# A transformer mixer on one core: the second MLP's mixed first weights made in the first MLP's last block and kept in DRAM

## Chip, cores and metric

The kernel runs on one core of a Trainium2 chip. The metric is the device time of one execution in microseconds (us); lower is better. TensorE (PE) does the matmuls, VectorE (DVE), ScalarE (ACT) and GpSimd (POOL) the elementwise work, SyncE (SP) issues nearly all DMAs.

## What is computed

Four sequences of 576 tokens, 8 heads of 64, in fp32. Windowed causal attention, then an MLP behind a layer norm, then a token mixer and a second MLP, each added to its input:

```python
attn = softmax(mask(q @ k.T / 8))            # each row sees itself and 63 keys before it
x  = (attn @ v) as [4, 576, 512]
x  = x + relu(layernorm(x) * g @ wa1) @ wa2  # wa1 512 x 2048, wa2 2048 x 512
u  = x + (relu(x.T @ tok1) @ tok2).T         # tok1 576 x 256, tok2 256 x 576, along the tokens
out = u + relu(u @ wb1) @ wb2                # wb1 512 x 1536, wb2 1536 x 512
```

## The kernel before, in words

**Numbers.** Every matmul operand is split into a high part (rounded to fp32r, on ScalarE) and a low part (source minus high, on VectorE or POOL); a product is three passes, `PASSES` (L358): high x high, high x low, low x high. `split` (L101) does both, `relu_split` (L360) does it behind a relu. The weights come as 64-bit values: `b_load` (L613) loads a piece of 512 KB into a raw buffer, `b_shrink` (L624) rescales its exponents on ScalarE, `b_narrow` (L630) makes fp32 of it by two VectorE instructions (L120, L121; the first into PSUM or, with `psum=False`, into SBUF) and loads the next piece into the raw buffer that came free. There are three raw buffers, parts of `qkv`, which held q, k and v of the attention.

**First MLP.** 18 tiles of 128 tokens in 6 blocks of 3. A block has 16 steps, one for each 128 hidden columns. `mm1` (L365) of step f makes the hidden values (12 matmuls of 384 columns into one of two PSUM banks of `ps_h`, then `relu_split`), `mm2` (L382) adds those of step f - 2 (`LAG` = 2) to three accumulators (9 matmuls of 512 columns). The weights of step f lie in SBUF slot f (`wslot`, L96, slots 0 to 15), so in the last block slot f comes free when `mm2` of f has run, in step f + 2. `hooks[f]` are functions called in step f between `mm1` and `mm2`, `hooks[f - 0.5]` ahead of the relu of step f. The order is written by hand: each engine takes its instructions in the order in which the program calls them, and a new tile in a slot waits for the readers of the old one.

**Last block (i = 5, L742 to L755), before.** Three pieces are loaded at step 0. The token rows `ys` (slots 0 to 4) are split at steps 3 to 7 by `ysk`, highs on ScalarE and lows on VectorE. From step 8 pieces are narrowed and split: tok1 in two (`t1_piece`), tok2 in two (`t2_piece`), rests of both (`rest_piece`), then wb1 and wb2 pieces alternating. `t2_piece` takes slot 6 + a, and clears its pads by memsets on POOL (L552) when its load is issued. At step 12 `mix_w1(0)` runs.

**Mixing.** The second MLP's first product is done on blocks of 2 x 2 with seven products in place of eight. For that each wb1 chunk q (of six) is needed in seven forms: a11, a12, a22 (`w1a`) and four sums m1 to m4 (`w1b`). `mix_w1` (L591) makes them of the narrowed chunk `atmp`: highs and lows of the three plain forms, four sums on VectorE (L598), highs and lows of the sums, and stores both tiles to DRAM (`kept`, L606), 768 KB and 1 MB. `load_w1` (L586) loads them back for the later pairs.

**Token mixing (L773 to L848).** `tok_up(b)` makes the hidden values of sequence b in two halves, with functions called in between, `tok_down(t)` gives tile t's result, which VectorE adds to x (L805). Order: up 0, up 1, down 0 to 8 (with the second half's `ys`, highs on ScalarE and lows on POOL), up 2, up 3, down 9 to 17. Meanwhile u of tiles 0 to 5 is transposed by VectorE in 32 x 32 blocks, 16 instructions for three tiles (`block_transpose`, L342), into two tiles `ut` (slots 15 and 11), and `x_steps` (L829) makes seven combinations of it (`xm`, subtractions on VectorE, then a split each); its first two steps run behind the second half of up 3, the others at down 10 to 14.

**Second MLP (L851 to L1006).** Three pairs of two blocks, each pair in six quads (q = 0 to 5), one for a wb1 chunk q and its wb2 chunk. `quad` (L884) runs seven products (six matmuls of 384 columns each, into two PSUM banks in turn, emptied by ScalarE or VectorE) and, from the second quad on, four `down` products (nine matmuls of 512 columns) of the quad before. `jobs[k]` are functions called at eight places in it. In the first pair (p = 0) job 0 of quad q calls `mix_w1(q + 1)`, and jobs 1, 2, 3 and 5 narrow pieces of wb1 and wb2 and split wb2; four places in slots 15 and 11 (`more`) serve as raw buffers. `turn` transposes the next pair's tiles on VectorE.

Of the kernel before, what the change touches and what calls it, by code (L numbers as in the profile page):

```python
# [68 lines left out]
def mixer_kernel(ctx, tc, qT, kT, v, g, wa1, wa2, tok1, tok2, wb1, wb2, out):  # L69
# [334 lines left out]
    with tc.manual_schedule():  # L404
# [104 lines left out]
        HALF = FB // 2  # L509
        W1_SLOT, W2_SLOT = ((8, 9), (5, 6)), (10, 7, 12, 13, 14, 11)  # L510
        w2, ws1, atmp = {}, {}, {}
        kept = dram.tile([HALF, P, 7 * DM], F32, name="kept")

        def new_ys(pr, k):
            ys[pr, k] = wslot(k, [P, 2, 2, DM], f"ys{pr}_{k}")

# [24 lines left out]
        def t1_piece(k):  # L541
            if k == 0:
                tw["t1"] = wslot(5, [P, 2, 4, T1], "t1")
# [18 lines left out]

        def w2_piece(q, k):
            def parts(w):
                if k == 0:
                    w2[q] = wslot(W2_SLOT[q], [P, 2, 2, DM], f"w2_{q}")
                return [(w, w2[q][:, k, 0], w2[q][:, k, 1])]
            f = q + k * HALF
            return [(ALLP, 0, DM, wb2[f * P:(f + 1) * P, :])], parts

        def w1_piece(q, k):
            f = q + k * HALF
            return [(ALLP, 0, DM, wb1[f * P:(f + 1) * P, :])], (q, k)

# [15 lines left out]

        def mix_w1(q):  # L591

            t_ = atmp.pop(q).rearrange("p k (c n) -> p (k c) n", c=2).bitcast(F32)
            a_, b_ = new_w1(q)
# [12 lines left out]
        pb = [(t1_piece, (k,)) for k in range(2)] + [(t2_piece, (a,)) for a in range(2)] + [(rest_piece, ())]  # L609
        pb += [(fn, (q, k)) for q in range(HALF) for fn in (w1_piece, w2_piece) for k in range(2)]  # L610
        todo_b, ready_b = list(enumerate(pb)), []

# [17 lines left out]
        def b_narrow(psum=True):  # L630
            b_shrink()
            _, k, raw, width, parts = ready_b.pop(0)
            if isinstance(parts, tuple):
                if parts[1] == 0:
                    atmp[parts[0]] = ap.tile([P, 2, DM], U32, tag="p", name=f"atmp{parts[0]}")
                tmp = atmp[parts[0]][:, parts[1]]
# [12 lines left out]
        def b_split():  # L649
            b_shrink()  # L650
# [155 lines left out]

        tok_up(0)
        tok_up(1)
        uts_ = [wslot(k, [P, KD, N], f"ut{i}", F32) for i, k in enumerate((15, 11))]
        parts = [lambda k=k, i=i: block_transpose(uts_[i], i, k) for i in range(2) for k in range(16)]  # L810

# [26 lines left out]

        tt = [ap.tile([P, 2, N], F32, tag="p", name=f"t{k}x") for k in range(2)]
        xs0 = x_steps(uts_[0], uts_[1], *tt, [nc.gpsimd, nc.gpsimd, nc.vector, nc.gpsimd, nc.vector, nc.gpsimd, nc.vector])  # L840
        tok_up(2, [lambda: run(3) for _ in range(4)])
        tok_up(3, [lambda: run(3), lambda: run(4), lambda: run(3), *xs0[0], *xs0[1], lambda: None, lambda: None])
        xm += [wslot(k, [P, 2, 2, N], f"xm{k}") for k in range(5)]
        for t in range(9, 18):
            tok_down(t)
            if 10 <= t < 15:
                for fn in xs0[t - 8]:
                    fn()  # L848


# [99 lines left out]
        for p in range(PAIRS):  # L950
            old, acc_of = acc, {}
            for q in range(HALF):
                n = p * HALF + q
                jobs = collections.defaultdict(list)
                if p == 0:
                    if q == 0:
                        more = [wslot(k, [P, 2, 2 * DM], f"more{k}", U32) for k in (15, 11)]
                        places = [more[k][:, h] for k in range(2) for h in range(2)]
                        order = [[places[k % 4]] for k in range(12)] + [places[0:1], places[1:2], [], places[0:1]]
                        rawb_of = lambda raw: order.pop(0) if order else []  # L960
                    if q < HALF - 1:
                        jobs[0].append(lambda q=q: mix_w1(q + 1))
                        for k in (1, 2):
                            jobs[k] += [lambda: b_narrow(False), b_split]
                        if q < HALF - 2:
                            for k in (3, 5):
                                jobs[k].append(lambda: b_narrow(False))
                if n + 1 >= HALF and n + 1 < PAIRS * HALF:
                    jobs[0].append(lambda n=n: load_w1(n + 1))
                if p < PAIRS - 1:  # L970
                    if q == 0:
# [10 lines left out]
                    if q == HALF - 1:  # L982
                        tx = wslot(15, [P, 2, 2, N], f"tx{p}", F32)
                        steps = x_steps(ux[:, 0], ux[:, 1], tx[:, 0], tx[:, 1], [nc.gpsimd, nc.vector] * 4)
                        for k in range(7):
                            jobs[k] += steps[k]
# [60 lines left out]
```

## Time and profile before

| what | us |
|---|---|
| median of 3 runs | 860.7 (858.77 to 862.88) |
| the profiled execution | 859.97 |
| its span, first to last instruction | 858.2 |
| TensorE busy in the span | 817.1 (95%) |
| VectorE, ScalarE, POOL busy | 572.4, 329.7, 165.4 |
| granted TensorE clock, mean | 0.982 |

All rows are of that one execution; times in a row that names a start count from the span's first instruction. A row with "[x <-ENGINE name]" says that the engine stood idle for x before it and what ended that. A merged row counts several instructions ("x9") from the first's start to the last's end. L numbers are lines of the kernel before.

### The profile page before, as it was taken

The numbers are of one execution on the slowest core, as the hardware profiler recorded it, in microseconds if no ns is written. First come the engines' busy times: TensorE is split into PE (matmuls) and PEld (weight loads), VectorE is DVE, ScalarE is ACT, GpSimd is POOL, SyncE is SP. The second block draws the span as 40 slices with busy tenths as digits, with TensorE's granted clock in tenths as the row PEclk, the third lists the DMA queues.
The fourth block names the chain that finished last, engine by engine and source line by source line (L and its number), as shares of the span: only waits on it lengthen the run. The fifth ranks groups of instructions, "written<-read, shape, count | busy, mean of one in ns | idle before, by whom it ended". The sixth has DMA issues, their size and how long they took to land.

```text
span 858.2 us, 13091 instructions
## 1 busy us (share of the span) xinstructions
PE 817.1 (95%) x4902; PEld 717.9 (84%) x4902; DVE 572.4 (67%) x1352; ACT 329.7 (38%) x844; POOL 165.4 (19%) x171
## 2 busy tenths in 40 slices
PE   8999999999999999999999987778889999999998
PEld 6888898898899898899998865666778889889896
DVE  6888768787786877776374597777787644742213
ACT  6887433334423334422353312533344222422221
POOL 3655300000000000000033403433333000310000
PEclk9999999999999999999999999799989999999999
DMA  9887111102201111200055000555432442244312
GB/s 344 259 293 242 56 62 50 57 2 77 82 1 56 57 56 38 97 27 0 1 167 184 1 0 12 209 184 179 146 153 87 160 172 86 93 151 173 106 67 74
DMA packets 28543, 91.41 MB, mean 107 GB/s; under 512 B 3392, under 2 KB 4416, under 8 KB 26176
## 3 DMA queue, kind: packets, MB, share of 16 engines
q1 hardware_dynamic: 28336, 90.32, 30.4%
q8 instruction: 38, 0.62, 0.3%
q10 hardware_dynamic: 144, 0.26, 0.1%
q14 instruction: 25, 0.20, 0.1%
HBM read 74.84 MB, written 15.73 MB: 106 GB/s over the span
## 4 chain that ended last, share of the span: by engine, by line
PE 81%; DVE 10%; ACT 3%; issue 2%; POOL 2%; DMA 1%; SPq 0%; DVEq 0%; POOLq 0%; ACTq 0%
PE acca L385 23%; PE ha L374 22%; PE accb L867 15%; PE prod L858 13%; PE o L281 2%; DVE ut L347 2%; PE s L188 2%; DVE atmp L598 1%; DVE tmpb L121 1%; PE td L802 1%; PE accb L1003 1%; DVE xs L805 1%; PE th L786 1%; DMA more<-in_wb 1%; POOL w L104 1%
## 5 line engine op out<-in xcount | busy, mean ns | idle before, releaser
L374 PE MATMUL ha<-xnt,wa 128*128 128x384 f32 x1152 | 216.8, 337 | 0.8 <-POOL wa L104 0.5
L385 PE MATMUL acca<-wa,hTa 128*128 128x512 f32 x864 | 215.5, 395 | 0.0
L374 PEld LDWEIGHTS ha<-xnt,wa 128*128 128x128 f32 x1152 | 203.9, 188 | 9.5 <-DVE xnt L339 1.2
L385 PEld LDWEIGHTS acca<-wa,hTa 128*128 128x128 f32 x864 | 159.3, 188 | 32.6 <-issue 2.4
L867 PE MATMUL accb<-w,hx 128*128 128x512 f32 x612 | 158.2, 404 | 0.2 <-DVE xs L941 0.2
L867 PEld LDWEIGHTS accb<-w,hx 128*128 128x128 f32 x612 | 118.3, 195 | 22.4 <-issue 0.5
L361 ACT ACTIVATE hTa<-ha 128x384 fp32r<-128x384 f32 x96 | 46.8, 488 | 217.9 <-PE ha L374 217.8
L362 DVE SCALAR_TENSOR_TENSOR hTa<-ha,hTa 128x384 fp32r<-128x384 f32 x96 | 53.3, 555 | 85.7 <-ACT hTa L361 84.8
L256 DVE STREAM_TRANSPOSE pts<-f 32x256 f32<-32x256 f32 x192 | 83.7, 436 | 3.1
L858 PE MATMUL prod<-xm,w1b 128*128 128x384 f32 x324 | 66.3, 348 | 11.6 <-ACT s L872 11.6
L858 PEld LDWEIGHTS prod<-xm,w1b 128*128 128x128 f32 x324 | 59.1, 193 | 17.5 <-ACT s L872 14.8
L881 DVE SCALAR_TENSOR_TENSOR hx<-s,hx 128x384 fp32r<-128x384 f32 x54 | 35.9, 665 | 45.8 <-ACT hx L878 45.4
L878 ACT ACTIVATE hx<-s 128x384 fp32r<-128x384 f32 x54 | 28.3, 524 | 90.9 <-PE accb L867 87.9
L872 ACT ACTIVATE s<-prod 128x384 f32<-128x384 f32 x72 | 34.7, 488 | 69.2 <-PE prod L858 58.7
L355 DVE STREAM_TRANSPOSE xhT<-xh 32x128 f32<-32x128 f32 x192 | 57.9, 301 | 2.8
L875 DVE TENSOR_TENSOR s<-prod,s 128x384 f32<-128x384 f32 x36 | 20.0, 556 | 58.2 <-PE prod L858 58.0
L858 PE MATMUL prod<-xm,w1a 128*128 128x384 f32 x216 | 47.1, 357 | 8.1 <-DVE s L875 8.1
L305 POOL TENSOR_SCALAR mv<-mv 128x1 f32<-128x1 f32 x13 | 2.6, 196 | 269.4 <-ACT xhT L304 269.3
L858 PEld LDWEIGHTS prod<-xm,w1a 128*128 128x128 f32 x216 | 41.2, 201 | 11.0 <-DVE s L875 9.4
L875 POOL TENSOR_TENSOR s<-s,s 128x384 f32<-128x384 f32 x18 | 19.3, 1073 | 153.8 <-ACT s L872 153.8
L104 POOL TENSOR_TENSOR wa<-tmp,wa 128x512 fp32r<-128x512 f32 x32 | 41.5, 1312 | 34.0 <-ACT wa L103 32.2
L209 ACT ACTIVATE f<-f,mx 128x128 f32<-128x128 f32 x120 | 46.3, 388 | 1.2 <-DVE mx L201 1.2
(165 smaller groups left out, 975.1 us busy)
## 6 DMA issues: line engine op xcount, KB each, us to landing
xs<-in_wa SPq DMA_DIRECT2D x32, 512.0 KB, 4.7
w1b<-kept SPq DMA_DIRECT2D x12, 1024.0 KB, 6.6
w1a<-kept SPq DMA_DIRECT2D x12, 768.0 KB, 4.5
more<-in_wb SPq DMA_DIRECT2D x15, 512.0 KB, 5.7
qkv<-in_v SPq DMA_DIRECT2D x28, 256.0 KB, 3.3
kept<-w1b SPq DMA_DIRECT2D x6, 1024.0 KB, 4.9
qkv<-in_wb SPq DMA_DIRECT2D x9, 512.0 KB, 4.6
kept<-w1a SPq DMA_DIRECT2D x6, 768.0 KB, 3.2
```

The lines of the kernel that those rows point to most:

```text
L104: lo_engine.tensor_tensor(out=dst_lo, in0=src, in1=dst_hi.bitcast(F32), op=ALU.subtract)
L209: nc.scalar.activation(out=f_[:, h], in_=f_[:, h], func=AF.Exp, scale=-1.0, bias=mx[:, h], accum_out=sm[:, h])
L256: nc.vector.transpose(out=s_[32 * b:32 * b + 32, :, 32 * a:32 * a + 32], in_=f_[32 * a:32 * a + 32, :, 32 * b:32 * b + 32])
L355: nc.vector.transpose(out=uts[t][32 * b:32 * b + 32, :, 32 * a:32 * a + 32], in_=s_)
L361: nc.scalar.activation(out=dst_hi, in_=src, func=AF.Relu)
L362: nc.vector.scalar_tensor_tensor(out=dst_lo, in0=src, scalar=0.0, in1=dst_hi.bitcast(F32), op0=ALU.max, op1=ALU.subtract)
L374: nc.tensor.matmul(h_, lhsT=w[:, a, c * P:(c + 1) * P], rhs=src[c][:, b], start=n == 0, stop=n == 3 * KD - 1)
L385: nc.tensor.matmul(acc[j], lhsT=t_[:, a, j * P:(j + 1) * P], rhs=ws[f][:, 2 + b], start=f == first and n == 0, stop=f == last and n == 2)
L858: nc.tensor.matmul(dst, lhsT=w_[:, a, c * P:(c + 1) * P], rhs=xm[m][:, c, b], start=first and n == 0, stop=n == 5, skip_group_check=True)
L867: nc.tensor.matmul(acc[j], lhsT=hx[role][:, a, (j % TPB) * P:(j % TPB + 1) * P], rhs=w2[q][:, k, b], start=q == 0 and role in ("21", "12") ...
L875: eng.tensor_tensor(out=dst, in0=x, in1=y, op=ALU.add)
L881: nc.vector.scalar_tensor_tensor(out=hx[role][:, 1], in0=src, scalar=0.0, in1=hx[role][:, 0].bitcast(F32), op0=ALU.max, op1=ALU.subtract)
```

## The change

The wb1 pieces come first: those of q = 2, 3, 4, 5, 0 (`ORDER`) before the token weights, that of q = 1 behind them, then all wb2 pieces. Three are loaded already in the block before the last (step 13). In the last block every step from 1 to 15 narrows one piece; `mix_w1` is now three functions at three successive steps: `w1_plain` (splits of a11, a12, a22 and the four sums, which go from VectorE to POOL), `w1_mixed` (split of the sums) and `w1_keep` (the store). They use slots 0 to 3. `ys` moves to slots 4 to 8 and to steps 7 to 11, tok1 to slot 9, tok2 to slots 10 and 11. q = 1 is mixed during up 1, and the first wb2 chunk is narrowed and split during up 3 and down 9 to 17. In the first pair W1 of q = 2 to 5 is loaded from DRAM; two narrows and one wb2 split are left in a quad, with two raw places. Of the six tiles' transposes for the first pair, three tiles stay with VectorE and three go to TensorE (`turn1`: 12 transposes of 128 x 128 and four copies on ScalarE). The turns for the next pair are spread as 10, 11, 11 over quads 2 to 4. Cut to its core:

```diff
-        W1_SLOT, W2_SLOT = ((8, 9), (5, 6)), (10, 7, 12, 13, 14, 11)
+        W1_SLOT, W2_SLOT = ((0, 1), (2, 3)), (9, 10, 11, 12, 13, 14)
...
-            t2[a] = wslot(6 + a, [P, 2, 960], f"t2_{a}")
+            t2[a] = wslot(10 + a, [P, 2, 960], f"t2_{a}")
...
-        def mix_w1(q):
+        def w1_plain(q):
+            t_ = wtmp["1", q].rearrange("p k (c n) -> p (k c) n", c=2).bitcast(F32)
+            a_, _ = new_w1(q)
             a11, a12, a21, a22 = (t_[:, k] for k in range(4))
-            sub = lambda out, x, y, op=ALU.subtract: nc.vector.tensor_tensor(out=out, in0=x, in1=y, op=op)
             split(a_[:, 2, 0], a_[:, 2, 1], a22, nc.gpsimd)
             split(a_[:, 0:2, 0], a_[:, 0:2, 1], t_[:, 0:2], nc.gpsimd)
-            sub(a22, a21, a22, ALU.add)
-            sub(a21, a11, a21)
-            sub(a11, a22, a11)
-            sub(a12, a12, a11)
+            for out_, x, y, op in ((a22, a21, a22, ALU.add), (a21, a11, a21, ALU.subtract),
+                                   (a11, a22, a11, ALU.subtract), (a12, a12, a11, ALU.subtract)):
+                nc.gpsimd.tensor_tensor(out=out_, in0=x, in1=y, op=op)
+        def w1_mixed(q):
+            t_ = wtmp.pop(("1", q)).rearrange("p k (c n) -> p (k c) n", c=2).bitcast(F32)
+            b_ = ws1[q][1]
             split(b_[:, :, 0], b_[:, :, 1], t_, nc.gpsimd)
+        def w1_keep(q):
             for x_, k_ in w1_rows(q):
                 nc.sync.dma_start(out=k_, in_=x_)
+        ORDER = (2, 3, 4, 5, 0)
+        pb = [(w_piece, (wb1, "1", q, k)) for q in ORDER for k in range(2)]
+        pb += [(t1_piece, (k,)) for k in range(2)] + [(t2_piece, (a,)) for a in range(2)] + [(rest_piece, ())]
+        pb += [(w_piece, (wb1, "1", 1, k)) for k in range(2)]
+        pb += [(w_piece, (wb2, "2", q, k)) for q in range(HALF) for k in range(2)]
...
+                if i == NBLOCKS - 2:
+                    hooks[FA - 3].append(lambda: b_load(3))
...
-                hooks[0].append(lambda: b_load(3))
                 for k in range(5):
-                    hooks[k + LAG + 1].append(lambda k=k: ysk(k))
-                for f in range(6 + LAG, 12 + LAG):
+                    hooks[k + LAG + 5].append(lambda k=k: ysk(k))
+                for f in range(1, FA):
                     hooks[f - 0.5] = [b_narrow]
-                    hooks[f].append(b_split)
-                    if f != 7 + LAG:
-                        hooks[f] += [b_narrow, b_shrink]
-                hooks[10 + LAG].append(lambda: mix_w1(0))
+                for k, q in enumerate(ORDER):
+                    for x, fn in enumerate((w1_plain, w1_mixed, w1_keep)):
+                        hooks[2 * k + 3 + x].append(lambda q=q, fn=fn: fn(q))
+                for f in range(FA):
+                    hooks[f] += [b_split, b_shrink] if f > 10 else [b_shrink]
...
-        tok_up(0)
-        tok_up(1)
+        tok_up(0, [b_split, lambda: b_narrow(), b_shrink, lambda: b_narrow()])
+        tok_up(1, [lambda: w1_plain(1), lambda: w1_mixed(1)])
...
+        turn1((0, 1))
+        tok_up(2, [lambda: turn1((2, 3)), lambda: run(3), lambda: run(3), b_shrink])
+        tok_up(3, [*xs0[0], *xs0[1], b_narrow, lambda: None, lambda: None, lambda: None])
...
+            if t == 12:
+                b_narrow()
+            if t == 15:
+                w2_split(0)
...
-                        jobs[0].append(lambda q=q: mix_w1(q + 1))
-                        for k in (1, 2):
-                            jobs[k] += [lambda: b_narrow(False), b_split]
-                        if q < HALF - 2:
-                            for k in (3, 5):
-                                jobs[k].append(lambda: b_narrow(False))
-                if n + 1 >= HALF and n + 1 < PAIRS * HALF:
+                        for k in (0, 2):
+                            jobs[k].append(b_shrink)
+                            jobs[k + 1].append(lambda: b_narrow(False))
+                        jobs[5].append(lambda q=q: w2_split(q + 1))
+                if 2 <= n + 1 < PAIRS * HALF:
                     jobs[0].append(lambda n=n: load_w1(n + 1))
...
-                        per = (0, 6, 6, 6, 14, 0) if p == 0 else (6, 7, 7, 6, 6, 0)
+                        per = (0, 0, 10, 11, 11, 0) if p == 0 else (6, 7, 7, 6, 6, 0)
```

## Rows read from the trace of the kernel before

**Rows 1.** Stretches: start:end, length; busy us (instructions) of each engine; PEclk, DMA share, GB/s.
```profile
400.50:467.35 66.85, 66.85 (x338) 60.65 (x337) 35.91 (x58) 25.98 (x50) 13.92 (x16) 1.00 0.34 113
467.35:530.90 63.55, 56.16 (x234) 43.99 (x233) 48.12 (x70) 15.79 (x25) 17.93 (x12) 0.97 0.00 1
530.90:549.03 18.13, 10.05 (x44) 9.41 (x42) 13.82 (x19) 8.19 (x16) 8.98 (x6) 0.81 0.55 203
549.03:571.56 22.53, 19.72 (x79) 16.86 (x79) 15.86 (x24) 8.71 (x17) 7.93 (x6) 0.85 0.51 186
...
639.62:655.91 16.29, 15.88 (x80) 13.95 (x78) 13.33 (x14) 9.49 (x16) 7.06 (x5) 1.00 0.33 119
...
687.92:703.62 15.70, 15.70 (x79) 14.14 (x78) 7.25 (x13) 4.03 (x9) 1.01 (x1) 1.00 0.33 122
```
**Rows 2.** Waits of TensorE, 467 to 656: total, times, longest.
```profile
PE prod L858 <- ACT s L872: 11.6, 8, 4.0
...
PE td L802 <- DVE xs L805: 6.4, 5, 3.5
```
**Rows 3.** Waits of ScalarE, 530 to 656.
```profile
ACT w1b L103 <- DVE atmp L598: 16.7, 5, 3.4
```
**Rows 4.** The chain that ended last: start, us; steps 13 and 15 of the last block.
```profile
452.82 2.08 PE acca L385 x9
...
459.09 2.10 PE ha L374 x12
```
**Rows 5.** Groups by line and form, VectorE, 394 to 660: busy, mean ns.
```profile
L362 DVE SCALAR_TENSOR_TENSOR hTa<-ha,hTa 128x384 fp32r<-128x384 f32 x17 | 9.5, 557 | 24.2 <-ACT hTa L361 24.1
...
L121 DVE SCALAR_TENSOR_TENSOR tmpb<-qkv,low 128x512 uint32<-128x512 uint32 x6 | 4.1, 688 | 0.7
```
**Rows 6.** The same for ScalarE, 394 to 660.
```profile
L111 ACT ACTIVATE qkv<-qkv 128x512 f32<-128x512 f32 x13 | 8.8, 674 | 0.8 <-DMA qkv<-in_tok 0.3 <-DMA qkv<-in_wb 0.3
L361 ACT ACTIVATE hTa<-ha 128x384 fp32r<-128x384 f32 x17 | 8.3, 490 | 35.5 <-PE ha L374 35.5
...
L103 ACT ACTIVATE w1b<-atmp 128x1024 fp32r<-128x1024 f32 x6 | 6.4, 1058 | 20.2 <-DVE atmp L598 20.2
```
**Rows 7.** The same for POOL, whole span.
```profile
L104 POOL TENSOR_TENSOR w1b<-atmp,w1b 128x1024 fp32r<-128x1024 f32 x6 | 14.8, 2462 | 17.6 <-issue 8.9 <-ACT w1b L103 8.7
...
L104 POOL TENSOR_TENSOR w1a<-atmp,w1a 128x512 fp32r<-128x512 f32 x6 | 7.7, 1286 | 0.0
...
L104 POOL TENSOR_TENSOR w1a<-atmp,w1a 128x256 fp32r<-128x256 f32 x6 | 4.4, 739 | 37.0 <-ACT w1a L103 37.0
```
**Rows 8.** Timeline of POOL in the last block: start, us, what, idle before.
```profile
434.03 0.35 POOL L552 MEMSET t<- 128x128 f32 x2 [52.54 <-PE acca L385]
438.22 0.36 POOL L552 MEMSET t<- 128x128 f32 x2 [3.84 <-PE acca L385]
438.53 5.05 POOL L104 TENSOR_TENSOR t<-tmpb,t 128x512 fp32r<-128x512 f32 x4
```
**Rows 9.** Timeline of ScalarE in the last block, first high of a token weight.
```profile
433.17 0.64 ACT L103 ACTIVATE t<-tmpb 128x512 fp32r<-128x512 f32 x1 [0.21 <-DVE tmpb L121]
```
**Rows 10.** Instructions of line 833 on VectorE: min/median/max ns, first and last start.
```profile
L833 DVE TENSOR_TENSOR tx<-qkv,tx x4: 945/946/946, 644.8 to 749.5; 128x768 f32<-128x768 f32 x4
...
L833 DVE TENSOR_TENSOR ut<-ut x1: 1984/1984/1984, 520.9 to 520.9; 128x768 f32<-128x768 f32 x1
```
**Rows 11.** POOL's lows of ys in the token mixing, likewise.
```profile
L104 POOL TENSOR_TENSOR ys<-xs,ys x8: 1289/1300/1747, 481.3 to 490.0; 128x512 fp32r<-128x512 f32 x8
```
**Rows 12.** Timeline of TensorE in the token mixing, after its longest wait.
```profile
515.55 4.60 PE L802 MATMUL td<-h,t 128*128 128x512 f32 x12 [3.49 <-DVE xs L805]
```
**Rows 13.** The page's slices: GB/s moved in each of 40.
```profile
GB/s 344 259 293 242 56 62 50 57 2 77 82 1 56 57 56 38 97 27 0 1 167 184 1 0 12 209 184 179 146 153 87 160 172 86 93 151 173 106 67 74
```
**Rows 14.** TensorE's transposes of 128 x 128 ahead of the first two blocks.
```profile
L321 PE MATMUL tpa<-ident,xh x24: 270/273/330, 20.3 to 102.1; 128*128 128x128 f32 x24
```
**Rows 15.** Timeline of VectorE in the token mixing.
```profile
508.65 4.66 DVE L347 STREAM_TRANSPOSE ut<-xs 32x384 f32<-32x384 f32 x8
```

More of the change, by code (lines that the diff above doesn't have):

```diff
@@ L561, in rest_piece, with w_piece @@
                      for a in range(2)])
[L563 to L567, printed above, removed]
+        def w_piece(src, what, q, k):
             f = q + k * HALF
[L569 to L573, printed above, removed]
+            return [(ALLP, 0, DM, src[f * P:(f + 1) * P, :])], (what, q, k)
         def new_w1(n):
@@ L589, in load_w1, with w2_split @@
                 nc.sync.dma_start(out=t_, in_=k_)
-        def mix_w1(q):
-            t_ = atmp.pop(q).rearrange("p k (c n) -> p (k c) n", c=2).bitcast(F32)
-            a_, b_ = new_w1(q)
+        def w1_plain(q):
+            t_ = wtmp["1", q].rearrange("p k (c n) -> p (k c) n", c=2).bitcast(F32)
+            a_, _ = new_w1(q)
             a11, a12, a21, a22 = (t_[:, k] for k in range(4))
-            sub = lambda out, x, y, op=ALU.subtract: nc.vector.tensor_tensor(out=out, in0=x, in1=y, op=op)
             split(a_[:, 2, 0], a_[:, 2, 1], a22, nc.gpsimd)
             split(a_[:, 0:2, 0], a_[:, 0:2, 1], t_[:, 0:2], nc.gpsimd)
-            sub(a22, a21, a22, ALU.add)
-            sub(a21, a11, a21)
-            sub(a11, a22, a11)
-            sub(a12, a12, a11)
+            for out_, x, y, op in ((a22, a21, a22, ALU.add), (a21, a11, a21, ALU.subtract),
[4 more added lines that the diff above has]
+            b_ = ws1[q][1]
             split(b_[:, :, 0], b_[:, :, 1], t_, nc.gpsimd)
+        def w1_keep(q):
             for x_, k_ in w1_rows(q):
                 nc.sync.dma_start(out=k_, in_=x_)
-        pb = [(t1_piece, (k,)) for k in range(2)] + [(t2_piece, (a,)) for a in range(2)] + [(rest_piece, ())]
-        pb += [(fn, (q, k)) for q in range(HALF) for fn in (w1_piece, w2_piece) for k in range(2)]
+        def w2_split(q):
+            t_ = wtmp.pop(("2", q)).bitcast(F32)
+            w2[q] = wslot(W2_SLOT[q], [P, 2, 2, DM], f"w2_{q}")
+            for k in range(2):
+                split(w2[q][:, k, 0], w2[q][:, k, 1], t_[:, k], nc.gpsimd)
+        ORDER = (2, 3, 4, 5, 0)
[3 more added lines that the diff above has]
+        pb += [(w_piece, (wb2, "2", q, k)) for q in range(HALF) for k in range(2)]
         todo_b, ready_b = list(enumerate(pb)), []
@@ L633, in b_narrow @@
             if isinstance(parts, tuple):
-                if parts[1] == 0:
-                    atmp[parts[0]] = ap.tile([P, 2, DM], U32, tag="p", name=f"atmp{parts[0]}")
-                tmp = atmp[parts[0]][:, parts[1]]
+                what, q, half = parts
+                if half == 0:
+                    wtmp[what, q] = ap.tile([P, 2, DM], U32, tag="p", name=f"wtmp{what}_{q}")
+                tmp = wtmp[what, q][:, half]
             else:
@@ L649, in b_split @@
         def b_split():
-            b_shrink()
             for parts, w in narrowed_b:
@@ L805, in tok_down @@
             nc.vector.tensor_tensor(out=xt[t], in0=p_, in1=xt[t], op=ALU.add)
-        tok_up(0)
-        tok_up(1)
-        uts_ = [wslot(k, [P, KD, N], f"ut{i}", F32) for i, k in enumerate((15, 11))]
-        parts = [lambda k=k, i=i: block_transpose(uts_[i], i, k) for i in range(2) for k in range(16)]
+        tok_up(0, [b_split, lambda: b_narrow(), b_shrink, lambda: b_narrow()])
+        tok_up(1, [lambda: w1_plain(1), lambda: w1_mixed(1)])
+        ut = wslot(15, [P, KD, N], "ut0", F32)
+        u1 = [hp.tile([P, 2, N], F32, tag="hT", name=f"ut1_{k}") for k in range(2)]
+        parts = [lambda k=k: block_transpose(ut, 0, k) for k in range(16)]
         def run(n):
@@ L839, in mixer_kernel, with turned, turn1 @@
         tt = [ap.tile([P, 2, N], F32, tag="p", name=f"t{k}x") for k in range(2)]
[L840 to L843, printed above, removed]
+        xs0 = x_steps(ut[:, 0:2], ut[:, 2:4], u1[0], u1[1], *tt,
+                      [nc.gpsimd, nc.gpsimd, nc.vector, nc.gpsimd, nc.vector, nc.gpsimd, nc.vector])
+        def turned(c):
+            nc.scalar.activation(out=u1[c // 2][:, c % 2], in_=tps.pop(c), func=AF.Copy)
+        def turn1(cs):
+            for c in cs:
+                trans_tiles("u", xt, 1, c, range(TPB))
+            for c in cs:
+                turned(c)
+        turn1((0, 1))
+        tok_up(2, [lambda: turn1((2, 3)), lambda: run(3), lambda: run(3), b_shrink])
+        tok_up(3, [*xs0[0], *xs0[1], b_narrow, lambda: None, lambda: None, lambda: None])
+        xm += [wslot(4 + k, [P, 2, 2, N], f"xm{k}") for k in range(5)]
         for t in range(9, 18):
@@ L956, in mixer_kernel @@
                     if q == 0:
-                        more = [wslot(k, [P, 2, 2 * DM], f"more{k}", U32) for k in (15, 11)]
-                        places = [more[k][:, h] for k in range(2) for h in range(2)]
-                        order = [[places[k % 4]] for k in range(12)] + [places[0:1], places[1:2], [], places[0:1]]
+                        more = wslot(15, [P, 2, 2 * DM], "more", U32)
+                        order = [[more[:, k]] if k >= 0 else [] for k in (0, 1, -1, 0, 1, 0, 1, 0)]
                         rawb_of = lambda raw: order.pop(0) if order else []
                     if q < HALF - 1:
-                        jobs[0].append(lambda q=q: mix_w1(q + 1))
-                        for k in (1, 2):
-                            jobs[k] += [lambda: b_narrow(False), b_split]
-                        if q < HALF - 2:
-                            for k in (3, 5):
-                                jobs[k].append(lambda: b_narrow(False))
-                if n + 1 >= HALF and n + 1 < PAIRS * HALF:
+                        for k in (0, 2):
[3 more added lines that the diff above has]
+                if 2 <= n + 1 < PAIRS * HALF:
                     jobs[0].append(lambda n=n: load_w1(n + 1))
@@ L983, in mixer_kernel @@
                         tx = wslot(15, [P, 2, 2, N], f"tx{p}", F32)
-                        steps = x_steps(ux[:, 0], ux[:, 1], tx[:, 0], tx[:, 1], [nc.gpsimd, nc.vector] * 4)
+                        steps = x_steps(*(ux[:, i, c:c + 2] for i in range(2) for c in (0, 2)), tx[:, 0], tx[:, 1],
+                                        [nc.gpsimd, nc.vector] * 4)
                         for k in range(7):
```

15 lines of the change are left out of this document (9 added, 6 removed).

## Prediction

> **What bounds the kernel now.** I read the page first: TensorE is busy 95% of the span, so time can only come back where it waits or runs at the low clock. The stretches [rows 1] show where that is. In the last block of the first MLP it is busy all 66.85 us at granted clock 1.00. In the token mixing it is busy 56.2 of 63.6. The six quads of the second MLP's first pair take 18.1, four times about 22.5 (the row shown and three more of 22.3 to 23.3) and 16.3, together 125.0 us (530.90 to 655.91), while an undisturbed quad, the one from 687.92, takes 15.70. The granted clock says the same: 0.81 in the first quad, between its levels of 1.2 GHz (0.5) and 2.4 GHz, and 1.00 in the undisturbed one. So the first pair holds some 38 us of loss, the token mixing 11, and nothing else holds much.
>
> The waits of TensorE [rows 2] name ScalarE's copy of a product and VectorE's token sum as releasers. Behind the copy stands ScalarE's own wait [rows 3]: 16.7 us in five places for VectorE's sums in the mixed weights (the old mix_w1 puts them behind POOL's lows of the unmixed ones). ScalarE works in order, so a copy queued behind that split holds the product that needs its PSUM bank. The mix is what stalls the first pair, and the change takes it out of there.
>
> **Last block: what the mix costs there.** Five of six weights (q = 2, 3, 4, 5, 0) are now narrowed at steps 1 to 10, split unmixed at steps 3, 5 .. 11, mixed at 4, 6 .. 12 and stored one step later. A step is 2.10 + 2.08 = 4.18 us of TensorE [rows 4], so a weight has two steps, 8.4 us.
> - VectorE, per step: a narrow 2 x 0.69 and the relu's low 0.56 [rows 5], with two lows of ys, 1.4, at four steps: at most 3.3 of 4.18.
> - ScalarE, per two steps: two relus 1.0, two shrinks 1.35 and the highs of the weight, 1.06 and at most twice 0.64 [rows 6, 9], with four highs of ys at 0.64: 7.3 of 8.4.
> - POOL, per weight: lows 1.29 + 0.74, the four sums, now on POOL, 4 x 0.74 (the row of a low of the same shape, likewise with two inputs in SBUF), and the mixed low 2.46 [rows 7]: 7.45 of 8.4. POOL becomes the tight engine, but until step 10 it fits.
>
> Then it meets a wait that moves with the token weights. Their zero pads are memsets on POOL, issued when a piece is loaded, and wait until the old weight in the slot has been read. Before, both memsets stood on POOL until TensorE had finished, 52.5 and 3.8 us, and the low of a token weight whose high was out at 433.8 started only behind the second, at 438.5 [rows 8, 9]. That cost nothing, as POOL had nothing else to do. Now the t2 pieces are pieces 12 and 13 and their slots 10 and 11, so the second memset stands in POOL's queue from step 11 until the accumulation of step 13 ends, at 454.9 [rows 4]. Behind it are the lows and sums of q = 0; behind these, on ScalarE, is its mixed high (step 12); behind that the split of t1, a shrink and relu 13; and with relu 13 the PSUM bank that the products of step 15 want at 459.1. From 454.9: memset 0.35, lows 2.03, sums 2.96, mixed high 1.06, t1 high 0.64, shrink 0.67, narrow 1.38, low 0.56, in all 9.65, so 464.55: **5.5 us** of stall.
>
> Two additions. VectorE's lows of ys (two SBUF inputs) now run beside POOL. A VectorE sum beside POOL's low took 1.98 instead of 0.95, and a POOL low met by one of VectorE's took 1.75 instead of 1.30 [rows 10, 11], while a narrow with one input in PSUM stayed at 0.69 [rows 5]. Eight lows at steps 7 to 10 and four at step 11 would cost between nothing and half of their 12 x 0.69 on POOL's chain; I take 1 us, nearer to nothing because only those behind step 9 reach the late part. And after a wait of 3.5 us TensorE ran 12 matmuls of 128x512 in 4.60 us [rows 12], where 2.08 for nine [rows 4] makes 2.8: 1.8 lost. Of two waits I take 1 us, as part of it lies under relu 15's chain. Sum for the block: **+7.5**, bounds 0 (the wait fits in the two steps that TensorE has in hand) and +15.
>
> The Trainium skill, page SBUF — State Buffer, section "Who interferes with whom", says that a VectorE instruction with two SBUF inputs and a GpSimd instruction that reads SBUF exclude each other for the whole instruction, whichever started first. Rows 10 and 11 show both directions of it. Without any such exclusion the sum below would be 826, with it as sized here 827, and taken in full it is the second rival.
>
> DMA in this block: a weight loads 2 x 0.52 MB and stores 1.84 MB in 8.4 us, 344 GB/s, as much as the best slice of the page [rows 13]. A load has two steps until its shrink and can stand behind one store of 1.84 MB, 5.3 us at that rate. I cost it at nothing; if that cover is gone it is a rival. The stores wait on SP for POOL's lows with the next load behind them, which has the same two steps.
>
> **Token mixing.** Sixteen of the 32 block transposes leave VectorE, 16 x 0.58 = 9.3 us (eight took 4.66) [rows 15]; twelve PE transposes come, at most 0.27 each [rows 14], 1.8 to 3.3 us, and four ScalarE copies of 0.5. Four narrows come to VectorE, 4 x 1.38 = 5.5; Net, VectorE loses 3.8 us. The mix of q = 1 comes to ScalarE and POOL ahead of the second ys. At 0.231 per matmul [rows 4] its highs start 9.7 us after the stage begins (42 matmuls); with 1.0 for highs, 5.0, 1.06 and 2.46 as above and four lows of ys at 1.30 [rows 11] the first ys of tok_up(2) stand at 24.4, and tok_up(2) begins at 26.8 (116 matmuls): covered, with 2.4 in hand; what exceeds that is on the path. In the second half it is the bound: it transposes for 4.66 us in one go from 508.65 [rows 15], after tok_up(3)'s first half, and only then the first subtraction may start. That start now lies under tok_up(3); the rest (nine token sums, three subtractions, three lows, two narrows, ScalarE's highs between) still runs slower than TensorE. I take -4.7 for these transposes and -0.9 for the first subtraction [rows 10], +1.4 for a narrow in the chain and +0.2 for what of the turned tiles isn't covered: **-4**; bounds -8 (all of 11 less the added work) and 0 (VectorE still as late).
>
> **First pair.** The quads lose the mix; they keep two narrows, two shrinks and a w2 split, and gain a load of W1 from DRAM, as the undisturbed quad has it [rows 1]. There VectorE is busy 7.25 us, seven turns among it; four more turns (2.3) and two narrows (2.8 at the price above) make 12.4 of 15.7. A W1 load has a whole quad to land, as it has there. No job sits within a window shorter than a down product, 2.08 [rows 4], so I take 15.8 each for four quads and leave the sixth at 16.3. The first has no down products: seven of six 128x384 matmuls, 7 x 1.05 = 7.4, plus the last wait for the relu's low and the w2 split, about 1.6: 9.0. Sum 9.0 + 63.2 + 16.3 = 88.5 against 125.0: **-36.5**, bounds -39 (every quad at its matmuls) and -26 (quads of 18).
>
> **Sum.** The profiled execution took 859.97 us (span 858.2); the median of the runs shown is 0.7 above it. 859.97 + 7.5 - 4 - 36.5 = **827.0**. A measurement here tells about 0.5%, 4.3 us, from no change.
>
> **Rivals.**
> 1. The block loses nothing: 859.97 - 40.5 = 819.5. For it, the two steps that TensorE runs ahead; against it, the 9.65 us chain behind the second memset. 0.12.
> 2. The port turns pace POOL: 37.3 us of its work and all 12 lows (8.3) in the ten steps 3 to 12 (41.8) make 3.8 more, with 5.5 of the memset and VectorE's own late lows 3, twice 1.8 of clock: 15.9, less 2 in common, 14: 833.5. For it rows 10 and 11; against it, lows fit while ScalarE keeps POOL waiting. It is the rule of the Trainium skill's page named above in full. 0.16.
> 3. DMA paces the block: at 259 GB/s, the page's second slice [rows 13], 2.88 MB take 11.1 us, 2.7 over two steps, five times 13.7, with the memset 5.5: +19, 838.5. Against it: the stores come in bursts with idle between. 0.09.
> 4. The quads stay at 18: turns, narrows and token splits hold a copy or a relu each time. Five times 2.2: 838. For it, ScalarE's order; against it, the free time counted above. 0.13.
> 5. Slower: TensorE waits out every mix in the last block. Run through alone a mix takes a high of 0.64, lows 2.03, sums 2.96, mixed high 1.06 and low 2.46, 9.15. Five of these with 1.8 of clock each are 55: 859.97 - 40.5 + 55 = 874.5. It decides from 9.0 us per weight, clock included ((40.5 + 4.3) / 5). Rows 3 speak for it (ScalarE waited for each mix), the two steps in hand against. 0.04.
> 6. The change leaves the mix in the first pair: the diff takes out the only call there. 0.01, 860.
>
> **How the numbers follow.** The forecast has 0.45. The likeliest case itself spans 820 to 834. The range goes up to rivals 3 and 4 with some room for their sizes and down to the block's and mixing's lower bounds together, 813 to 844; what is left out is rival 5, half of the upper bounds of 3 and 4 and a few hundredths below. Faster 0.45 + 0.12 + 0.16 + 0.09 + 0.13 = 0.95, of which I move 0.01 to no change with rival 6: 0.94, 0.02, 0.04.
>
> **What would show it.** Right: quads of about 15.7 from the second on, the first near 9; no wait of ScalarE for a mix behind 531; POOL's second memset ending near 455 with q = 0's lows behind it, and TensorE waiting 3 to 7 us at step 15; the token mixing near 59 us with VectorE still the releaser of td. Wrong: TensorE busy through step 15 (rival 1), lows of ys or POOL sums over 1.2 us at steps 7 to 11 (2), shrinks waiting for DMA (3), products waiting in quads two to five (4), a wait at each even step (5).

## The result and the profile after

The changed kernel takes 825.9 us (825.57 to 827.15, 4 runs) against 860.7 before: ratio 0.9598, 95% interval 0.9572 to 0.9623. The forecast was 827.0. The profiled execution took 825.79 with a span of 824.0, 34.2 below that of before.

First the stretches of the changed kernel, cut as in [rows 1]: last block, token mixing (in two parts, at the first down product of its second half), then quads one, two, three and six of the first pair. Columns as there.

```profile
400.18:473.32 73.14, 68.69 (x337) 61.80 (x336) 43.26 (x62) 33.92 (x64) 46.13 (x46) 0.98 0.64 230
473.32:514.00 40.68, 40.68 (x186) 33.47 (x185) 28.84 (x43) 15.82 (x28) 20.04 (x16) 1.00 0.20 76
514.00:532.14 18.14, 14.57 (x61) 10.91 (x60) 15.12 (x19) 6.37 (x10) 8.51 (x6) 1.00 0.29 87
532.14:541.67 9.53, 7.51 (x44) 7.18 (x42) 6.69 (x11) 6.00 (x12) 4.26 (x4) 1.00 0.25 81
541.67:558.98 17.31, 17.31 (x78) 15.76 (x79) 6.31 (x10) 5.71 (x12) 4.13 (x4) 0.90 0.40 131
558.98:574.69 15.71, 15.71 (x80) 14.14 (x78) 11.41 (x20) 6.20 (x13) 3.52 (x3) 1.00 0.54 187
606.10:622.43 16.33, 15.87 (x79) 13.95 (x77) 12.98 (x13) 9.49 (x16) 7.11 (x5) 1.00 0.34 119
```

Against [rows 1] the block is 6.3 us longer (73.14 for 66.85), the mixing 4.7 shorter (58.82 for 63.55), and the first pair 34.7 shorter (532.14 to 622.43, 90.3, for 125.0). These make -33.1 of the -34.2; of the rest, 0.7 lies in the two later pairs (201.6 us from 622.43 to the end, 202.3 before). Quads three to six are at their matmuls but for half a us in the last. POOL's busy time in the block has gone from 13.9 to 46.1 us.

What TensorE still waits for, 395 to 660 (total, times, longest), beside [rows 2]; the wait for a product's copy is gone:

```profile
PE ha L374 <- DVE hTa L362: 4.4, 2, 3.3
PE td L807 <- DVE xs L810: 3.6, 3, 1.6
PE prod L883 <- DVE hx L906: 2.5, 2, 2.0
```

The two waits of 4.4 us are in the last block. The timelines of POOL, ScalarE and TensorE there (start, us, instruction, idle before):

```profile
442.22 3.90 POOL L592 TENSOR_TENSOR wtmp<-wtmp 128x256 f32<-128x256 f32 x4
450.62 0.35 POOL L552 MEMSET t<- 128x128 f32 x2 [4.50 <-PE acca L385]
450.93 2.41 POOL L104 TENSOR_TENSOR w1b<-wtmp,w1b 128x1024 fp32r<-128x1024 f32 x1
454.81 0.35 POOL L552 MEMSET t<- 128x128 f32 x2 [1.47 <-PE acca L385]
455.12 1.97 POOL L104 TENSOR_TENSOR w1a<-wtmp,w1a 128x256 fp32r<-128x256 f32 x2
457.05 3.20 POOL L592 TENSOR_TENSOR wtmp<-wtmp 128x256 f32<-128x256 f32 x4
```
```profile
451.27 0.48 ACT L361 ACTIVATE hTa<-ha 128x384 fp32r<-128x384 f32 x1
460.28 1.06 ACT L103 ACTIVATE w1b<-wtmp 128x1024 fp32r<-128x1024 f32 x1 [8.53 <-POOL wtmp L592]
```
```profile
450.39 2.27 PE L374 MATMUL ha<-xnt,wa 128*128 128x384 f32 x12
...
455.92 2.38 PE L374 MATMUL ha<-xnt,wa 128*128 128x384 f32 x12 [1.17 <-DVE hTa L362]
...
463.66 3.66 PE L374 MATMUL ha<-xnt,wa 128*128 128x384 f32 x12 [3.27 <-DVE hTa L362]
```

POOL finishes q = 5's sums at 446.1 and stands for TensorE twice; the second memset ends at 455.2, the lows and sums of q = 0 behind it at 460.2, and ScalarE, which has nothing else that it may do first, stands 8.53 us before the mixed high. The products of step 15 then wait 3.27 us and run 3.66 in place of 2.27 (the row at 450.39, of a step without a wait): the granted clock of that stretch (463.66 to 467.32) is 0.61, near its level of 1.2 GHz.

### The profile page after: what moved, and what is told of

It is laid out like the page before. It is cut to its first block, busy times and chain, and to the rows that moved or that the text cites. A ratio compares the mean times of both kernels' runs of the same rounds, so it can differ in the third digit from the quotient of the medians.

```text
span 824.0 us, 13148 instructions
## 1 busy us (share of the span) xinstructions
PE 803.8 (98%) x4914; PEld 710.7 (86%) x4914; DVE 542.2 (66%) x1312; ACT 331.6 (40%) x848; POOL 186.3 (23%) x195
## 4 chain that ended last, share of the span: by engine, by line
PE 85%; DVE 6%; POOL 3%; issue 2%; ACT 2%; DMA 1%; SPq 0%; DVEq 0%; POOLq 0%; ACTq 0%
PE acca L385 22%; PE ha L374 22%; PE accb L892 17%; PE prod L883 16%; PE o L281 2%; PE s L188 2%; PE td L807 1%; POOL wtmp L592 1%; DVE ut L347 1%; PE accb L1026 1%; POOL w1a L104 1%; PE th L791 1%; DMA kv<-in_kT 1%; DVE xs L810 1%; DVE hx L906 1%
## 5 line engine op out<-in xcount | busy, mean ns | idle before, releaser
L892 PE MATMUL accb<-w,hx 128*128 128x512 f32 x612 | 152.6, 393 | 0.2 <-DVE xs L966 0.2
L892 PEld LDWEIGHTS accb<-w,hx 128*128 128x128 f32 x612 | 113.9, 188 | 21.2 <-issue 0.5
L906 DVE SCALAR_TENSOR_TENSOR hx<-s,hx 128x384 fp32r<-128x384 f32 x54 | 38.2, 708 | 52.5 <-ACT hx L903 52.5
L883 PE MATMUL prod<-xm,w1b 128*128 128x384 f32 x324 | 62.7, 338 | 0.0
L883 PE MATMUL prod<-xm,w1a 128*128 128x384 f32 x216 | 43.5, 337 | 0.0
L883 PEld LDWEIGHTS prod<-xm,w1a 128*128 128x128 f32 x216 | 38.6, 188 | 1.5
```

Source lines behind the costliest of these rows:

```text
L883: nc.tensor.matmul(dst, lhsT=w_[:, a, c * P:(c + 1) * P], rhs=xm[m][:, c, b], start=first and n == 0, stop=n == 5, skip_group_check=True)
L892: nc.tensor.matmul(acc[j], lhsT=hx[role][:, a, (j % TPB) * P:(j % TPB + 1) * P], rhs=w2[q][:, k, b], start=q == 0 and role in ("21", "12") ...
L906: nc.vector.scalar_tensor_tensor(out=hx[role][:, 1], in0=src, scalar=0.0, in1=hx[role][:, 0].bitcast(F32), op0=ALU.max, op1=ALU.subtract)
```

## The experiments

Ratios are to the kernel before, timed on the same chip. The changed kernel was timed again beside the first three.

> The changed kernel again, as the measure for the other runs of this chip: 825.9 us, 825 to 828 by every theory.

825.55 us, ratio 0.9598 (0.9583 to 0.9612), span 824.0.

**The memsets at the split.**

```diff
-            for z in (512, 640):
-                nc.gpsimd.memset(t2[a][:, :, z:z + 64].bitcast(F32), 0.0)
-            return ([(ALLP, 0, DM, tok2[a * P:(a + 1) * P, 0:DM])],
-                    lambda w: [(w, t2[a][:, 0, 0:DM], t2[a][:, 1, 0:DM])])
+            def cleared(w):
+                for z in (512, 640):
+                    nc.gpsimd.memset(t2[a][:, :, z:z + 64].bitcast(F32), 0.0)
+                return [(w, t2[a][:, 0, 0:DM], t2[a][:, 1, 0:DM])]
+            return [(ALLP, 0, DM, tok2[a * P:(a + 1) * P, 0:DM])], cleared
```

> The changed kernel, with the two pads of tok2 cleared when the piece is split (steps 13 and 14) and not when it is loaded (steps 10 and 11), so that POOL no longer stands for TensorE with q = 0's lows and sums behind it. My theory (the memset's place in POOL's queue makes most of the block's loss of 6 us): TensorE's wait ahead of step 15 (3.3 us) and the slow matmuls behind it (1.4 us) go, the block ends 4 to 6 us earlier, 820 to 822 us in all. Rival (POOL and VectorE taking turns at the port, or POOL's load of work as such, makes the loss): POOL is behind anyway, the gain is under 1.5 us, 824.5 to 826.5.

820.46 us, ratio 0.9538 (0.9521 to 0.9555). POOL's timeline around q = 0, then TensorE's only wait left in the block and the mixing's first product:

```profile
447.03 2.41 POOL L104 TENSOR_TENSOR w1b<-wtmp,w1b 128x1024 fp32r<-128x1024 f32 x1 [1.17 <-ACT w1b L103]
449.58 2.70 POOL L104 TENSOR_TENSOR w1a<-wtmp,w1a 128x256 fp32r<-128x256 f32 x2
452.24 3.96 POOL L594 TENSOR_TENSOR wtmp<-wtmp 128x256 f32<-128x256 f32 x4
...
461.02 0.36 POOL L554 MEMSET t<- 128x128 f32 x2
```
```profile
456.03 2.36 PE L374 MATMUL ha<-xnt,wa 128*128 128x384 f32 x12 [1.52 <-DVE hTa L362]
468.57 3.33 PE L793 MATMUL th<-ys,t 128*128 128x512 f32 x14
```

The lows of q = 0 start at 449.6 in place of 455.1, the wait ahead of step 15 is gone with its slow matmuls, and the mixing starts at 468.57 in place of 473.32. The block, which began at 399.94 here and at 400.18 there, is 4.5 us shorter (68.63 for 73.14), and the whole is 5.1 faster. So the memset's place in POOL's queue made 4.5 of the block's 6.3 us; POOL's load as such did not make these, for POOL does the same work here.

**The sums back on VectorE.**

```diff
-                nc.gpsimd.tensor_tensor(out=out_, in0=x, in1=y, op=op)
+                nc.vector.tensor_tensor(out=out_, in0=x, in1=y, op=op)
```

> The changed kernel, with the four sums of each weight back on VectorE (one part of the change undone). My theory: VectorE, in order, then waits at steps 3, 5 .. 11 for POOL's lows with the narrow and the relu's low of the next step behind it, and behind the memset it does so up to 457; ScalarE's mixed high comes 1.5 us earlier, but the relu's lows come later: slower by 1 to 6 us, 827 to 832. Rival (POOL is the engine that paces the block, so 16 us of sums taken off it help): 821 to 824.

828.65 us, ratio 0.9632 (0.9615 to 0.9649). VectorE's timeline at the place, and TensorE's wait:

```profile
448.13 2.77 DVE L537 TENSOR_TENSOR ys<-xs,ys 32x512 fp32r<-32x512 f32 x4
455.88 3.86 DVE L592 TENSOR_TENSOR wtmp<-wtmp 128x256 f32<-128x256 f32 x4 [4.97 <-POOL w1a L104]
```
```profile
461.65 4.21 PE L374 MATMUL ha<-xnt,wa 128*128 128x384 f32 x12 [6.90 <-DVE hTa L362]
```

VectorE stands 5 us for POOL's lows of q = 0, which stand behind the memset, and TensorE 6.9 at once. ScalarE's mixed high came no earlier (460.1 for 460.3, where 1.5 earlier was expected), since the first of the sums took until POOL's lows were done. Moving the sums to POOL is worth 3.1 us in this order of things; what it would be worth with the memsets late wasn't tried.

**The turned tiles back on VectorE.**

```diff
-        turn1((0, 1))
-        tok_up(2, [lambda: turn1((2, 3)), lambda: run(3), lambda: run(3), b_shrink])
-        tok_up(3, [*xs0[0], *xs0[1], b_narrow, lambda: None, lambda: None, lambda: None])
+        tok_up(2, [lambda: run(3), lambda: run1(0), lambda: run(3), b_shrink])
+        tok_up(3, [*xs0[0], *xs0[1], b_narrow, lambda: run1(1), lambda: None])
```

(`run1(h)` is 16 block transposes of half of the columns on VectorE.)

> The changed kernel, with tiles 3 to 5 transposed by VectorE in 32 half-size block transposes (about 12 us, an estimate from the 0.57 us of the whole size and 0.30 of a third of it) in place of TensorE's 12 and ScalarE's four copies. My theory (VectorE bounds the token mixing's second half, and the turned tiles are what lets the subtractions start under tok_up(3)): the mixing grows by 5 to 10 us, 831 to 836. Rival (the mixing's gain comes from the order of the steps, and VectorE had room for the transposes): within 1.5 us of the changed kernel, 824.5 to 827.5.

838.9 us, ratio 0.9756 (0.9734 to 0.9777): 13.4 slower, more than my range. The transposes in its trace, and TensorE's longest waits in the mixing:

```profile
L854 DVE STREAM_TRANSPOSE ut<-xs 32x192 f32<-32x192 f32 x32 | 11.8, 369 | 0.4
```
```profile
515.74 5.99 PE L791 MATMUL king_offset=None)_1_5282<-ys,t 128*128 128x512 f32 x14 [5.13 <-DVE h L362]
...
531.28 6.03 PE L807 MATMUL td<-h,t 128*128 128x512 f32 x18 [5.45 <-DVE xs L810]
```

The 11.8 us were sized right. They stand in two rows of 16, 6.1 us each, one ahead of a relu's low and one ahead of the token sums, and TensorE's two long waits (5.13 and 5.45) are behind these two places; behind each wait the matmuls also ran slow (14 in 5.99 us, where 3.3 is normal). That last part I left out. The rival falls for the transposes as they are placed here; spread singly over the mixing they weren't tried, and VectorE is busy 55.8 of its 72.95 us in this run.

**The w2 splits one quad later.**

```diff
-                        jobs[5].append(lambda q=q: w2_split(q + 1))
+                if p == 0 and q > 0:
+                    jobs[5].append(lambda q=q: w2_split(q))
```

> The changed kernel, with the split of wb2 chunk q + 1 (two highs on ScalarE, two lows on POOL) moved from job 5 of quad q to job 5 of quad q + 1, so that it is out of the first quad, whose relu splits have no down products to hide under. My theory (the first quad's last wait, 2.0 us for the relu's low, and the half-speed products behind it, 2 us, come from VectorE's lows standing beside POOL's w2 lows and from ScalarE's highs ahead of the relus): 1 to 4 us faster, 822 to 825. Rival (the chain copy, sum, relu, low of a quad without down products is as long by itself, or the two narrows make it): under 0.8 us, 825 to 826.7.

826.6 us, ratio 0.9613 (0.9594 to 0.9632), span 824.1: nothing gained, as the rival has it, but for another reason. Its quads one, two and six:

```profile
532.17:541.08 8.91, 7.48 (x44) 7.16 (x42) 6.07 (x11) 4.96 (x10) 1.76 (x2) 1.00 0.26 77
541.08:556.89 15.81, 15.81 (x78) 14.24 (x79) 5.69 (x10) 5.69 (x12) 3.52 (x3) 1.00 0.44 152
604.01:622.52 18.51, 15.87 (x79) 13.95 (x77) 14.28 (x14) 10.71 (x18) 11.94 (x7) 1.00 0.42 156
```

The first two quads gain 2.1 us (24.7 for 26.8), within the theory's 1 to 4. Of its two causes the traces show one: the relus' highs on ScalarE start where they did (539.22 and 539.24), but one of VectorE's lows, first of the changed kernel, then of this run, is no longer held beside POOL's w2 lows:

```profile
539.99 1.16 DVE L906 SCALAR_TENSOR_TENSOR hx<-s,hx 128x384 fp32r<-128x384 f32 x1
```
```profile
540.01 0.54 DVE L906 SCALAR_TENSOR_TENSOR hx<-s,hx 128x384 fp32r<-128x384 f32 x1
```

The sixth loses 2.2, in a wait of TensorE for a relu's low ahead of the next pair (2.64 us, 0.46 in the changed kernel): the last split now stands beside the next pair's subtractions and splits.

**Both together.**

> Both late memsets and late w2 splits. If the two losses lie one after the other on TensorE's path, the gains add up: my theory 817 to 821. Rival (the token mixing is paced by VectorE and takes up what the block gives back): no better than the w2 splits alone, 822 to 825.

822.27 us, ratio 0.9562 (0.9541 to 0.9583), span 819.3, where the late memsets alone gave 819.4 (the medians, from two chips, lie 1.8 apart, but the profiled execution was the slowest of four there and the fastest of four here). The quads are those of the run above (8.91, 15.82 and 18.50), so this is no sign that the mixing takes up what the block gives back: it starts at 468.55 and the first quad at 527.36, both earlier by what the block gained. The number fits the rival, its cause doesn't.

**One mix back in the first pair.** On top of the late memsets; the last block makes four weights, and quad 4 (the fifth, as q counts from 0) mixes q = 5.

```diff
-        ORDER = (2, 3, 4, 5, 0)
+        ORDER = (2, 3, 4, 0)
...
+                        if q == 4:
+                            jobs[0] += [lambda: w1_plain(5, nc.vector), lambda: w1_mixed(5), lambda: w1_keep(5)]
```

(Also: wb1's two pieces of q = 5 ahead of wb2's fifth chunk, three narrows in quads 2 and 3, no load of q = 5; in the block nothing is narrowed at steps 9 and 10, and q = 0 is mixed two steps earlier.)

> Late memsets, and the mix of one weight (q = 5) put back into the first pair: its two pieces are narrowed in quads 2 and 3 and mixed and stored at the start of quad 4, sums on VectorE as before the change; the last block makes four weights. My theory (a mix in the first pair holds TensorE's copies for about 7 us, a mix in the last block costs next to nothing): quad 4 takes 21 to 24 us in place of 15.7, the whole 5 to 8 us more than with late memsets alone, 825.5 to 830 if those give 821. Rival (the first pair was slow for the four narrows in a quad, its raw places and loads, not for the mix): quads 2 and 3 grow and quad 4 stays under 18, the whole within 3 us.

826.55 us, ratio 0.9611 (0.9582 to 0.964), span 825.9, 6.5 more than with late memsets alone (6.1 by the medians). Quads three, four and five:

```profile
554.99:571.26 16.27, 15.87 (x80) 13.95 (x78) 13.05 (x22) 7.24 (x14) 3.75 (x3) 1.00 0.50 174
...
571.26:587.04 15.78, 15.78 (x78) 14.22 (x79) 13.16 (x24) 6.25 (x13) 1.81 (x2) 1.00 0.66 242
587.04:608.06 21.02, 17.55 (x80) 15.39 (x78) 16.04 (x25) 7.84 (x16) 10.10 (x8) 0.92 0.26 99
```

The quad with the mix takes 21.0, those with a third narrow 16.3 and 15.8. In it ScalarE waits for VectorE's sums as in [rows 3]:

```profile
ACT w1b L103 <- DVE wtmp L594: 3.3, 1, 3.3
```

So the mix costs 5.3 us in its quad, and a third narrow 0.6 at most. A quad of before lost 6.8 (22.5 for 15.7), so the mix makes the larger part of it; the fourth narrow and the second split of those quads weren't tried. The block with a weight less is no shorter (69.1 us for 68.63): taking one mix out of it gave nothing back.

**Only the first split moved.** On top of the late memsets.

```diff
-                        jobs[5].append(lambda q=q: w2_split(q + 1))
+                        if q == 1:
+                            jobs[2].append(lambda: w2_split(1))
+                        if q > 0:
+                            jobs[5].append(lambda q=q: w2_split(q + 1))
```

> Late memsets, and of the w2 splits only that of q = 1 moved, out of the first quad into job 2 of the second; the others stay where the changed kernel has them, so that no split comes into the sixth quad. Theory after the run with all splits late (there the first two quads gained 2.1 us and the sixth lost 2.2, where the split stands beside the next pair's subtractions): the first two quads take 24.7 us in place of 26.9, the sixth stays at 16.3, 817.5 to 819.5 us in all. Rival (the second quad, which now holds two splits, gives the gain back): 820 to 821.

818.83 us, ratio 0.9518 (0.9504 to 0.9533). Its first two quads:

```profile
527.15:536.07 8.92, 7.48 (x44) 7.16 (x42) 6.08 (x11) 4.96 (x10) 1.79 (x2) 1.00 0.25 73
536.07:551.89 15.82, 15.82 (x79) 14.25 (x80) 7.87 (x10) 6.73 (x14) 7.03 (x5) 1.00 0.42 151
```

24.7 us, as expected, and the second quad carries two splits at its matmul time.

**Tile 8's lows at step 13.**

```diff
-                    hooks[k + LAG + 5].append(lambda k=k: ysk(k))
+                    hooks[k + LAG + (5 if k < 4 else 7)].append(lambda k=k: ysk(k))
```

> The same, and tile 8's rows of ys split at step 13 in place of step 11. Theory (TensorE's 1.5 us wait ahead of step 14 comes from VectorE's four lows of these rows, two SBUF inputs each, which stand beside POOL and ahead of relu 12's low): that wait goes, 816 to 818 us. Rival (the wait is ScalarE's: relu 12 stands behind the mixed high of q = 5 and the highs of q = 0): no change, 817.5 to 819.5.

819.1 us, ratio 0.9518 (0.9504 to 0.9533): no change. But the wait moved with the lows. VectorE, then TensorE:

```profile
457.59 4.87 DVE L537 TENSOR_TENSOR ys<-xs,ys 32x512 fp32r<-32x512 f32 x4
```
```profile
464.50 3.93 PE L385 MATMUL acca<-wa,hTa 128*128 128x512 f32 x16 [1.54 <-DVE hTa L362]
```

The wait ahead of step 14 is gone, and one of the same size stands near the end of the block. So the lows are its cause and ScalarE is not, though their new place costs the same.

**One low a step.**

```diff
-                        y_split(t, nc.vector)
+                        y_split(t, nc.vector if t < 8 else None)
+                for part in range(4):
+                    hooks[12 + part].append(lambda part=part: y_rest_low(8, part))
```

> As the run with the late memsets and the first split moved, but tile 8's four lows of ys spread over steps 12 to 15, one each, in place of all four at step 11 (with all four at step 13 the 1.5 us wait of TensorE followed them to the end of the block). Theory (the wait is the four lows in a row, 4.9 us of VectorE beside POOL where they take 0.69 each alone, ahead of one relu's low): spread, each fits into its step and the wait goes, 816.5 to 818 us. Rival (any place of them in the block costs it, as steps 12 to 15 are full): 818.5 to 820.

817.43 us, ratio 0.9509 (0.9496 to 0.9523), the fastest version here. TensorE's waits from 398 to 660 and the block's stretch:

```profile
PE td L811 <- DVE xs L814: 3.6, 3, 1.6
PE prod L887 <- DVE hx L910: 1.9, 2, 1.4
PE accb L896 <- DVE xs L970: 0.2, 1, 0.2
```
```profile
400.00:466.72 66.72, 66.72 (x335) 60.19 (x334) 41.46 (x61) 33.86 (x64) 47.86 (x46) 1.00 0.71 243
```

TensorE doesn't wait in the block at all. With five weights mixed in it the block takes 67.1 us from its first product (399.61) to the mixing's; before the change it took 66.85 [rows 1] with one.

## Why the prediction was right, step by step

That 827.0 came within 1.1 us of the measured time is in part luck. The mechanisms of the three terms hold, but the gain of the first pair was forecast 1.8 too large; against it the block's loss was 1.2 too large, the mixing's gain 0.7 too small, and 1.1 us came from stretches that no term named.

**The first pair** (-36.5 forecast, -34.7 measured). The mechanism holds: one mix put back costs 5.3 us in its quad. Five mixes left the pair, 26.5 of the 34.7 at that price (an estimate); how the rest divides between narrows, splits and raw places no run shows. The term was 1.8 too large, and the step that was off is "15.8 each for four quads" with 9.0 for the first. Quads three to five took 15.7; the first took 9.53 and the second 17.31, at granted clock 0.90. I had the w2 split in the sum of the first quad, but not that the wait of 2.0 us behind it is followed by slow products. With that split moved the two took 8.92 and 15.82, the terms as forecast.

**The last block** (+7.5 forecast, +6.3 measured). The chain behind the second memset was forecast to start at 454.9 and to hold step 15 until 464.55; it started at 454.8, and step 15 started at 463.66. The stall was sized 5.5 and measured 3.3: TensorE came to step 15 at 460.4 and not at 459.1, as it had already stood 1.17 ahead of step 14, and the chain took 8.9 in place of 9.65. The clock was sized 1 and measured 1.4 (3.66 for 2.27). That the memset makes the wait at step 15, and not POOL's load, is shown by the late memsets: 4.5 of the 6.3 went, with the same work on POOL. The Trainium skill, page PSUM — Partial Sum Buffer, section "Engine vs sequencer instructions", says that the queues of ScalarE, VectorE and GpSimdE are strictly first in, first out; the 4.50 and 1.47 us of POOL above agree.

**The port** (1 us in that sum, and rival 2). Here are VectorE's lows of ys in the block, first of the kernel before (POOL idle), then of the changed one (min/median/max ns):

```profile
L104 DVE TENSOR_TENSOR ys<-xs,ys x8: 683/690/693, 412.0 to 425.2; 128x512 fp32r<-128x512 f32 x8
L537 DVE TENSOR_TENSOR ys<-xs,ys x4: 680/684/684, 428.8 to 430.9; 32x512 fp32r<-32x512 f32 x4
```
```profile
L104 DVE TENSOR_TENSOR ys<-xs,ys x8: 681/1226/1324, 428.6 to 443.5; 128x512 fp32r<-128x512 f32 x8
L537 DVE TENSOR_TENSOR ys<-xs,ys x4: 679/683/2799, 449.0 to 451.1; 32x512 fp32r<-32x512 f32 x4
```

Seven of the eight lows took 1.06 to 1.32 us for 0.69, and one of the four small ones took 2.8 us, beside POOL's mixed low of 2.41; the other three (0.68) ran while POOL still stood for TensorE. POOL lost less, and ahead of the memset, where it stood idle afterwards: its sums took 0.81 on the mean, where 0.74 was taken. On the path this was the wait ahead of step 14, 1.2 to 1.5 us, which followed the four lows when they moved and went when they were spread (the block from 68.65 to 67.11 us, the whole from 818.83 to 817.43 on two chips). I had put the loss on POOL's chain; it was on VectorE's. Of rival 2 the sign was there that I had named for it, lows of ys over 1.2 us (the median is 1.226); it priced the port at 14 with the rest, and falls by size, not by kind.

**The token mixing** (-4 forecast, -4.7 measured). The first subtraction began at 512.3, under tok_up(3), as forecast; VectorE is still the releaser, 3.6 us in three waits for 6.4 in five. With the same three tiles turned by VectorE, in two rows of 16, the mixing took 73 us (472.96 to 545.91). That run shows that the way of turning matters; how the 4.7 divides between the transposes, the earlier subtraction and the narrows it doesn't show.

**The rivals.** Rival 1 (no loss in the block) was the last run's, not the change's. Rival 3 (DMA): no wait of ScalarE for a transfer in the block, though the stores' median landing went from 4.9 us to 7.3 for the larger ones; the two steps of cover held. Rival 4 (quads at 18) holds for one quad. Rival 5 (each mix waited out): ScalarE did wait for POOL's sums five times, 18.4 us in all, as its order had it, but 8.5 of that stood behind the memset, and the others passed under the two steps that TensorE has in hand. Rival 6: no mix is left behind 531. The waits of ScalarE, 400 to 474, for rivals 3 and 5:

```profile
ACT w1b L103 <- POOL wtmp L592: 18.4, 5, 8.5
ACT hTa L361 <- PE ha L374: 17.7, 10, 4.3
ACT t L103 <- DVE tmpb L121: 0.8, 2, 0.4
```

## What to carry to other kernels

Preparation that stalls a stage with short buffers can cost nothing in an earlier one that runs two steps ahead; price it there by the tightest engine's time per step, and then walk every queue for an instruction that waits for something else. A memset that clears a reused slot is such an instruction: in an idle queue it may wait for 50 us unseen, and once work stands behind it the same wait is on the path, so it belongs where its slot is free and not where the load is issued. An instruction moved out of one crowded place must be looked up in the place that it comes to, at both ends of the loop.

## What I had not expected

A wait of TensorE of 2 us was followed by slow matmuls in one place and not in another. Ahead of the second quad of the changed kernel TensorE waited 2.02 us, and six products took 2.29 us, where those behind the 1.44 us of the run with the first split moved took 1.33; the granted clock of the quad was 0.90 in the one and 1.00 in the other. So 0.6 us off that wait brought back a further 1.5. But the kernel before has the same wait without any loss behind it (second line):

```profile
541.67 2.29 PE L883 MATMUL prod<-xnt,w1a 128*128 128x384 f32 x6 [2.02 <-DVE hx L906]
```
```profile
579.00 1.31 PE L858 MATMUL prod<-xm,w1b 128*128 128x384 f32 x6 [2.03 <-ACT s L872]
```

What tells the two apart these runs don't show. And the one of VectorE's instructions of 32 partitions that met a low of POOL's was held by it as those of 128 were (2.8 us for 0.68).
